# Two tap buffers, a later scan, an earlier start to the last tiles, and two moves in the head

## The chip, the cores and the metric

One core of a Trainium2 chip runs the kernel. The metric is the device time of one execution in microseconds (us), as the median of several runs; lower is better. The five engines are named as the profile names them: PE multiplies matrices (PEld is its weight load), ACT is the scalar engine, DVE the vector engine, POOL is GpSimd, and SP only issues transfers and waits.

## The reference

Two branches work on the same input `x` (2048 rows of 512) and are mixed row by row by a gate:

```python
g = sigmoid((x * gate_w).sum(-1, keepdims=True))
qkv = x @ wqkv                                   # 32 heads of 16
a = softmax(q @ k.T * 16 ** -0.5) @ v @ wo       # full attention, no mask
# b: a state-space convolution with 128 complex states per channel
K = einsum("dn,dnl,dn->dl", C, exp(dt * A * l), dt * B).real   # taps
b = irfft(rfft(u, 2L) * rfft(K, 2L))[:L] + u * Dskip           # u is x
out = g * a + (1 - g) * b
```

## The kernel before, in words

**Attention.** The scores are never stored. The loop `for q in range(NQ)` has 512 steps: 32 groups (a quarter of the rows and four heads), each with 16 key tiles. One step `q` computes four score products (`qk`, PE, into one of three double PSUM banks `SC`), two exponentials of 128x1024 (`ex(2q)` and `ex(2q+1)`, ACT, from `SC` into a ring of seven slots `ET`), and four products with the values (`pv`, PE, into the PSUM bank `OA`). `VE` holds the values, 17 columns a head, the 17th column is one, so that `OA` gets the sums of the softmax too; for that `VE` is filled with 1.0 before the values are written over it. After 16 steps `norm` (DVE) transposes `OA`, divides, and every second time writes a piece of `OnT`, the left operand of the output projection. So the kernel has 1,024 exponentials, all on ACT, and everything else is meant to run beside them.

**The convolution** is cut into 32 chunks of 64 rows and 16 blocks of 32 channels:
- `table` (DVE) makes two blocks' powers at a time into `PT` (two buffers), and sends them to DRAM (`ptd`).
- `qload` reads a block back transposed (`Qt`, a DMA transpose).
- `kstage` (PE, DVE) makes the taps of a block in the PSUM bank `MB`, copies them with zeros around them to the staging buffer `Kst` (two DVE instructions, L796 and L797), and sends that to DRAM (`kpd`). There is one `Kst` before.
- `sstage` (PE, DVE) makes the chunk states of a block, four banks one after the other in `MB`, each copied to `Sst` (L820, L822) and sent to DRAM (`sd`).
- `sload` reads the states of a block transposed into `SG0` or `SG1` (a quarter of the channels, four blocks, each).
- `scan` (DVE) runs over the 31 chunks of a quarter; five instructions for each, the first one (L861) copies from `SG` and so waits for its four loads.
- `ystage` (PE, DVE) computes 32 units of output in `MB` from `Py`, `Tt` (read back from `ptd` and `kpd` by `yload`) and `SG`, and copies them to `Yst`.
- `combine` and `outs` make output tiles 0 to 11 inside the loop; tiles 12 to 15 need the last group of heads and come behind it.

**What sets the order.** Every engine runs its own list of instructions in order. The lists are written by a recorder: one step `q` after the other, and within a step first the attention, then `sch.step(rate)`, which lets the threads above go on as far as they may. A thread yields conditions: `("PE", cost)` and `("DVE", cost)` take from a budget that each step refills (1.65 for DVE, 0.62 for PE in most of the loop), `("AFTER", name, n)` holds until `n` steps behind the step in which `name` was marked, and `("LOCK", "MB")` holds the one bank that `kstage`, `sstage`, `ystage`, `outs` and the projections share. This decides only an order; the real waits are semaphores that the recorder derives from who reads and writes which buffer. So an instruction that waits holds up all that stands behind it on its engine. SP issues all transfers of the loop, in the order of the recorded steps, the DMA transposes of `Qt`, `SG` and `Yl` among them.

**Head.** x rows 0 to 511 come by `x0n` and are transposed on PE (with the identity `idb`) into `xT`; the first K and Q projections, the first score products and the first exponential follow. The state-space parameters begin beside it (`ssm_head`, the same ACT).

Of the kernel before, what the change touches and what calls it, by code (L numbers as in the profile page):

```python
# [244 lines left out]
def declare(nc, es):  # L245
    B = {}

    def sb(name, free, dt=BF16):
        B[name] = Buf(name, "sb", free, dt)
# [30 lines left out]
    sb("Dpb", 16)  # L280
    sb("Dp", 16, FP32)
    sb("Yl", 16 * D)
    sb("fo", 2 * D)

    for n in ("AreT", "AimT", "BreT", "BimT", "CreT", "CimT", "ldt", "dt"):
        sb(n, D)
# [22 lines left out]
    sb("tt2", 2 * CB * 16)  # L309
    sb("Qt", 2 * 32 * 128)  # L310
    sb("Sst", 4 * 512)
    sb("Kst", 8 * P)

    sb("SG0", 33 * 2 * 128)
    sb("SG1", 33 * 2 * 128)
# [87 lines left out]
def dap(t, off, dims):  # L403
    return bass.AP(tensor=t, offset=off, ap=[list(d) for d in dims])


def record(nc, p, B, ins):
# [3 lines left out]
    OA, MB = B["OA"], B["MB"]  # L411
# [11 lines left out]
    def load(eng, b, src, W, dims=None, off=0):  # L423
        dma(eng, lambda e: e.dma_start(b(off, dims), src()), [], W)
# [22 lines left out]
    for c in range(1, 4):
        load_xT(c)
# [4 lines left out]
    for a in range(4):  # L453
# [7 lines left out]
    idf, idb, x0n = B["idf"], B["idb"], B["x0n"]  # L461
    op("POOL", lambda g: g.iota(idf(0, [[1, P]]), [[1, P]], base=0, channel_multiplier=-1,
                                allow_small_or_imprecise_dtypes=True), [], [(idf, 0)])
    op("POOL", lambda g: g.memset(VE(0, [[1, 16 * 560]]), 1.0), [], [(VE, k) for k in range(16)])
    wm = B["wm"]
    op("DVE", lambda v: v.memset(wm(0, [[1, D]]), 0.0), [], [(wm, 0)])
    op("DVE", lambda v: v.tensor_scalar(idb(0, [[1, P]]), idf(0, [[1, P]]), 0.0, None, ALU.is_equal), [(idf, 0)], [(idb, 0)])
    for k in range(6):
        mm(lambda: SC[2](0, [[1, 512]]), lambda: wm(0, [[1, 128]]), lambda: wm(0, [[1, 512]]), [(wm, 0)], [(SC[2], 0, "warm")])
    op("DVE", lambda v: v.memset(hpi(0, [[1, 1]]), HALF_PI), [], [(hpi, 0)])  # L470
    op("DVE", lambda v: v.memset(pio(1, [[1, 1]]), 0.0), [], [(pio, 1)])
# [76 lines left out]
    def norm(b):  # L548
        qc, pi, w = b // 8, (b % 8) // 2, b % 2
        o = 0  # L550
        op("DVE", lambda v: v.transpose(OT(o, [[1, 512]]), OA(0, [[1, 512]])), [(OA, 0, b)], [(OT, 0, b)])  # L551
        op("DVE", lambda v: v.reciprocal(Rz(16 * w, [[1, 16]]), OT(o + 16, [[32, 16]])), [(OT, 0, b)], [(Rz, w)])
        op("DVE", lambda v: v.tensor_tensor(ON(16 * w, [[32, 16], [1, 16]]), OT(o, [[32, 16], [1, 16]]),
                                            Rz(16 * w, [[1, 16], [0, 16]]), ALU.mult), [(OT, 0, b), (Rz, w)], [(ON, w)])
        if w == 1:
            op("DVE", lambda v: v.transpose(OnT[qc](pi * 512, [[1, 512]]), ON(0, [[1, 512]])), [(ON, 0), (ON, 1)],
               [(OnT[qc], 0)])


    def tt(eng, o, a, b_, f, R, W):  # L560
# [5 lines left out]
    def key(*ns):  # L566
        return [(B[n], 0) for n in ns]
# [210 lines left out]

    kpd, Kst = B["kpd"], B["Kst"]

    op("POOL", lambda g: g.memset(Kst(0, [[1, 8 * P]]), 0.0), [], [(Kst, "z")])

    def kstage(blk):
        yield ("AFTER", f"pt{blk}", 1)
        yield ("AFTER", "wb", 1)
        yield ("AFTER", "Dp", 1)
        yield ("LOCK", "MB")
        o = (blk % 2) * PTN
        for part, wn in ((0, "wrb"), (1, "nwi")):
            yield ("PE", .6)  # L790
            for a in range(4):
                mm(lambda a=a: MB(0, [[1, 512]], 32 * a, 32), lambda wn=wn: B[wn](CB * blk, [[1, 32]]),
                   lambda a=a, part=part: PT(o + part * CB * T + 512 * a, [[1, 512]]), [(PT, blk % 2, blk), (B[wn], 0)],
                   [(MB, 0, ('K', blk))], part == 0, part == 1, pos=(0, 32 * a))
        yield ("DVE", .7)
        op("DVE", lambda v: v.tensor_copy(Kst(63, [[P, 8], [1, T]]), MB(0, [[T, 8], [1, T]])), [(MB, 0, ('K', blk)), (Kst, "z")], [(Kst, 0, blk)])  # L796
        op("DVE", lambda v: v.tensor_scalar(Kst(63, [[P, 8]]), MB(0, [[T, 8]]), B["Dp"](blk, [[1, 1]]), None, ALU.add),  # L797
           [(MB, 0, ('K', blk)), (B["Dp"], 0)], [(Kst, 0, blk)])
        sch.unlock("MB")
        dma("SP", lambda e: e.dma_start(kpd.dram(blk * P * 8 * P, [[8 * P, P], [1, 8 * P]]), Kst(0, [[1, 8 * P]])),  # L800
            [(Kst, 0, blk), (Kst, "z")], [(kpd, blk)])
# [45 lines left out]
    def scan():  # L847
# [234 lines left out]
    for q in range(NQ):  # L1082
# [36 lines left out]
    while sch.thr:
        p.q += 1  # L1120
        sch.step(dict(PE=1e3, DVE=1e3, POOL=1e3))
        assert p.q < NQ + 3000, [t[1] for t in sch.thr]
# [38 lines left out]
```

## Time and profile before

| what | value |
|---|---|
| median of 3 runs | 1101.4 us (1099.38 to 1102.48) |
| the profiled execution, its own time | 1103.83 us |
| its span, first to last instruction | 1102.0 us |
| ACT busy | 981.1 us (89%) |
| PE busy | 756.7 us (69%) |
| DVE busy | 634.8 us (58%) |
| POOL busy | 10.2 us (1%) |
| mean granted TensorE clock | 0.61 of 2.4 GHz |

The profiled execution lies 2.4 us above the median of the runs, of which 1.8 us are outside its span. Shares of busy time are means over a head, a loop with very different stages, and a tail. The rows of the trace show each place apart.

### The profile page before, as it was taken

What the parts mean: (1) busy time and instruction counts of PE and PEld (TensorE: products, weight loads), DVE (VectorE), ACT (ScalarE), POOL (GpSimd) and SP (SyncE); (2) the same over time, 40 slices, a digit from 0 to 9 for tenths busy, and PEclk for the clock granted to TensorE, in tenths of its full rate; (3) what the DMA queues carried; (4) which work ended last, traced back from release to release, by engine and by line L of the source; (5) the groups of instructions that cost most, each with busy time, mean ns of one, the idle gap of its engine ahead of it and who ended that gap; (6) DMA issues with size and microseconds to landing.
All of it is one profiled execution on the core that took longest, in us unless ns stands there. A gap on an engine that the chain in (4) does not pass through costs nothing.

```text
span 1102.0 us, 16304 instructions
## 1 busy us (share of the span) xinstructions
PE 756.7 (69%) x6614; PEld 211.7 (19%) x6614; DVE 634.8 (58%) x1354; ACT 981.1 (89%) x1042; POOL 10.2 (1%) x12
## 2 busy tenths in 40 slices
PE   6867667667566674666656648885877888877665
PEld 2211112111111111111111113332322333311111
DVE  6738889976549975399864521107968951131201
ACT  5999999998779987899888959995997999999995
POOL 3000000000000000000000000000000000000000
PEclk9988985555555556555566655555555555568856
DMA  8700000036580036800347562354464334100000
GB/s 167 154 1 1 1 1 1 1 111 176 134 229 21 1 107 143 227 22 1 106 105 211 151 175 73 85 130 94 105 125 104 85 89 94 38 17 24 20 1 20
DMA packets 227403, 92.17 MB, mean 84 GB/s; under 512 B 191872, under 2 KB 215040, under 8 KB 225280
## 3 DMA queue, kind: packets, MB, share of 16 engines
q1 hardware_dynamic: 224016, 88.90, 32.5%
q10 hardware_dynamic: 3312, 2.23, 1.0%
q8 instruction: 52, 0.85, 0.3%
q14 instruction: 23, 0.19, 0.1%
HBM read 27.92 MB, written 35.65 MB: 58 GB/s over the span
## 4 chain that ended last, share of the span: by engine, by line
ACT 43%; DVE 30%; PE 11%; SPq 8%; DMA 5%; issue 2%; ACTq 0%; DVEq 0%; POOL 0%; POOLq 0%
ACT ET L536 42%; PE MB L420 5%; DVE G L871 4%; SPq L773 4%; PE SC L420 4%; DVE s L864 3%; DVE s L866 3%; DVE s L869 3%; DVE SG L873 3%; DMA gm_kpd<-Kst 2%; DVE tt L561 2%; PE OA L420 2%; SPq L841 2%; DMA gm_sd<-Sst 2%; DVE OT L551 1%
## 5 line engine op out<-in xcount | busy, mean ns | idle before, releaser
L536 ACT ACTIVATE ET<-SC 128x1024 bf16<-128x1024 f32 x1024 | 966.2, 1109 | 98.3 <-PE SC L420 97.3
L420 PE MATMUL SC<-Qm,KT 32*128 32x512 bf16 x2048 | 289.6, 556 | 204.5 <-ACT ET L536 198.2
L420 PE MATMUL OA<-ET,VE 128*32 128x512 bf16 x2048 | 287.6, 565 | 1.3 <-ACT ET L536 1.2
L420 PEld LDWEIGHTS SC<-Qm,KT 32*128 32x128 bf16 x2048 | 54.6, 97 | 407.6 <-ACT ET L536 391.0
L420 PEld LDWEIGHTS OA<-ET,VE 128*32 128x32 bf16 x2048 | 53.8, 101 | 190.3 <-issue 184.0
L420 PE MATMUL MB<-Qt,X 64*32 64x256 bf16 x512 | 39.9, 404 | 70.6 <-DVE Kst L797 44.5
L551 DVE STREAM_TRANSPOSE OT<-OA 128x512 f32<-128x512 f32 x32 | 23.8, 743 | 88.2 <-PE OA L420 88.2
L931 DVE CAST Yst<-MB 128x256 bf16<-128x256 f32 x32 | 13.4, 418 | 101.0 <-PE MB L420 101.0
L561 DVE TENSOR_TENSOR tt<-B,D 128x1024 bf16<-128x1024 bf16 x96 | 62.0, 688 | 1.3
L420 PE MATMUL MB<-Py,SG 128*32 128x64 bf16 x1024 | 59.8, 314 | 2.3 <-issue 2.3
L796 DVE CAST Kst<-MB 128x512 bf16<-128x512 f32 x16 | 11.0, 689 | 82.5 <-DMA gm_kpd<-Kst 70.4
L820 DVE CAST Sst<-MB 128x256 bf16<-128x256 f32 x64 | 27.0, 422 | 53.3 <-PE MB L420 48.9
L871 DVE TENSOR_TENSOR G<-s,s 128x256 f32<-128x256 f32 x120 | 53.2, 444 | 4.1
L420 PE MATMUL MB<-Tt,X 64*32 64x64 bf16 x512 | 35.6, 267 | 27.9 <-DVE Yst L931 27.9
L864 DVE TENSOR_TENSOR s<-G,MU 128x256 f32<-128x256 f32 x120 | 52.8, 440 | 0.1
L866 DVE TENSOR_TENSOR s<-G,MU 128x256 f32<-128x256 f32 x120 | 52.6, 438 | 0.0
L869 DVE TENSOR_TENSOR s<-s,SG 128x256 f32<-128x256 f32 x120 | 51.9, 432 | 0.0
L420 PEld LDWEIGHTS MB<-Py,SG 128*32 128x32 bf16 x1024 | 42.8, 222 | 10.5 <-issue 2.5
L873 DVE CAST SG<-G 128x256 bf16<-128x256 f32 x120 | 36.1, 301 | 4.1
L420 PEld LDWEIGHTS MB<-Tt,X 64*32 64x32 bf16 x512 | 19.0, 135 | 82.3 <-issue 82.1
L561 DVE TENSOR_TENSOR PT<-tt,tt 128x1024 bf16<-128x1024 bf16 x48 | 33.2, 691 | 1.5
L561 DVE TENSOR_TENSOR ft<-FP,L 128x1024 f32<-128x1024 f32 (+1 forms) x32 | 33.7, 1085 | 0.4
(119 smaller groups left out, 419.4 us busy)
## 6 DMA issues: line engine op xcount, KB each, us to landing
gm_ptd<-PT SPq DMA_DIRECT2D x16, 1024.0 KB, 5.2
Py<-gm_ptd SPq DMA_DIRECT2D x32, 512.0 KB, 4.4
gm_sd<-Sst SPq DMA_DIRECT2D x64, 128.0 KB, 2.5
gm_kpd<-Kst SPq DMA_DIRECT2D x16, 256.0 KB, 2.6
Tt<-gm_kpd SPq DMA_DIRECT2D x128, 32.0 KB, 3.5
gm_xrd<-in_A_x_dram SPq DMA_DIRECT2D x1, 2048.0 KB, 12.5
X<-gm_xrd SPq DMA_DIRECT2D x8, 256.0 KB, 5.1
gm_ytd<-Yst SPq DMA_DIRECT2D x32, 64.0 KB, 1.8
```

Source lines behind the costliest of these rows:

```text
L420: op("PE", lambda t: t.matmul(out(), lhsT(), rhs(), start=start, stop=stop, skip_group_check=True, **kw), R, W)
L536: op("ACT", lambda a: a.activation(ET(1024 * e, [[1, 1024]]), sc(0, [[1, 1024]]), AF.Exp, scale=DH ** -0.5), [(sc, 0, h // 2), (sc, 1, h / ...
L551: op("DVE", lambda v: v.transpose(OT(o, [[1, 512]]), OA(0, [[1, 512]])), [(OA, 0, b)], [(OT, 0, b)])
L561: op(eng, lambda v: v.tensor_tensor(o(), a(), b_(), f), R, W)
L773: dma("SP", lambda e: e.dma_start_transpose(Qt((blk % 2) * PTN, [[128, 32], [1, 128]]), ptd.dram(blk * P * PTN, [[PTN, P], [1, PTN]])), [( ...
L820: op("DVE", lambda v, bank=bank: v.tensor_copy(Sst(512 * bank, [[256, 2], [1, 128]]), MB(0, [[256, 2], [1, 128]])), [(MB, 0, ('S', blk, ba ...
L841: dma("SP", lambda e: e.dma_start_transpose(sg(256 + CB * bl, [[128, 64], [1, CB]]), sd.dram(CB * blk * 8192, [[8192, CB], [1, 8192]])), [ ...
L864: op(e, lambda v: v.tensor_tensor(s2(0, [[128, 2], [1, 128]]), G(0, [[128, 2], [1, 128]]), MU(d0, [[0, 2], [1, 128]]), ALU.mult), key("G", ...
L866: op(e, lambda v: v.tensor_tensor(s3(0, [[128, 2], [1, 128]]), G(128, [[-128, 2], [1, 128]]), MU(D + d0, [[D, 2], [1, 128]]), ALU.mult), k ...
L869: op(e, lambda v, so=so: v.tensor_tensor(s2(0, [[1, 256]]), s2(0, [[1, 256]]), sg(so, [[1, 256]]), ALU.add), [(s2, 0)] + ks, [(s2, 0)])
L871: op(e, lambda v: v.tensor_tensor(G(0, [[1, 256]]), s2(0, [[1, 256]]), s3(0, [[1, 256]]), ALU.add), [(s2, 0), (s3, 0)], [(G, 0)])
L873: op(e, lambda v, so=so: v.tensor_copy(sg(so, [[1, 256]]), G(0, [[1, 256]])), key("G"), ks)
```

## The change

It has five parts.
1. `Kst` gets a second buffer: block `blk` uses half `blk % 2`. `kstage` starts three steps behind the table of its block, where it was one.
2. `scan` starts a quarter twelve steps behind the issue of the quarter's last `SG` load, where it was four.
3. Output tiles 12 to 15: the first three of their four partial products are issued before the last group is finished, in the bank `MB` and in banks of `SC`; the fourth follows behind the last `norm`. `fo`, from which the tiles are sent out, has four buffers, where it had two. Each piece of `OnT` is tracked apart. What is left of the threads is run out inside step 511.
4. The loads of `Wv` and of the later columns of `Wk` and `Wq` are issued by SP, between its transposes, where ACT issued them.
5. In the head, `VE` is filled by DVE, where POOL did it; PE gets nine warming products, where it had six; K's first evacuation is done by DVE behind `Qm`, where ACT did it.

```diff
-    sb("fo", 2 * D)
+    sb("fo", 4 * D)
-    sb("Kst", 8 * P)
+    sb("Kst", 2 * 8 * P)
...
-    load_w("Wv", 2 * D, 0, D, 0)
-    load_w("Wk", D, P, D - P, 1)
-    load_w("Wq", 0, P, D - P, 1)
     load_par("AreT", ins["are"])
     load_par("AimT", ins["aim"])
-    for c in range(1, 4):
-        load_xT(c)
+    load_w("Wv", 2 * D, 0, D, 0, "SP")
+    load_xT(1)
+    load_w("Wk", D, P, D - P, 1, "SP")
+    load_w("Wq", 0, P, D - P, 1, "SP")
+    load_xT(2)
+    load_xT(3)
...
-    op("POOL", lambda g: g.memset(VE(0, [[1, 16 * 560]]), 1.0), [], [(VE, k) for k in range(16)])
     op("DVE", lambda v: v.memset(wm(0, [[1, D]]), 0.0), [], [(wm, 0)])
     op("DVE", lambda v: v.tensor_scalar(idb(0, [[1, P]]), idf(0, [[1, P]]), 0.0, None, ALU.is_equal), [(idf, 0)], [(idb, 0)])
-    for k in range(6):
+    op("DVE", lambda v: v.memset(VE(0, [[1, 16 * 560]]), 1.0), [], [(VE, k) for k in range(16)])
+    for k in range(9):
...
-    op("POOL", lambda g: g.memset(Kst(0, [[1, 8 * P]]), 0.0), [], [(Kst, "z")])
+    op("POOL", lambda g: g.memset(Kst(0, [[1, 16 * P]]), 0.0), [], [(Kst, "z")])
...
-        yield ("AFTER", f"pt{blk}", 1)
+        yield ("AFTER", f"pt{blk}", 3)
...
-        op("DVE", lambda v: v.tensor_copy(Kst(63, [[P, 8], [1, T]]), MB(0, [[T, 8], [1, T]])), [(MB, 0, ('K', blk)), (Kst, "z")], [(Kst, 0, blk)])
+        op("DVE", lambda v: v.tensor_copy(Kst(1024 * (blk % 2) + 63, [[P, 8], [1, T]]), MB(0, [[T, 8], [1, T]])), [(MB, 0, ('K', blk)), (Kst, "z")], [(Kst, blk % 2, blk)])
...
-                yield ("AFTER", f"sg{4 * qr + bl}", 4)
+                yield ("AFTER", f"sg{4 * qr + bl}", 12)
...
-    proj_ev("K", 0, 0, mb, True)
...
     op("DVE", lambda v: v.tensor_scalar(Qm(0, [[1, 512]]), OA(0, [[1, 512]]), msk(0, [[1, 1]]), None, ALU.mult),
        [(OA, 0, ('p', "Q", 0, 0)), (msk, 0)], [(Qm, 0, 0)])
+    proj_ev("K", 0, 0, mb)
...
+    p.q = max(p.q, NQ)
+    banks = [(MB, 0, 0), (SC[(2 * NQ - 3) % 3], 0, 0), (SC[(2 * NQ - 3) % 3], 512, 1), (SC[(2 * NQ - 2) % 3], 0, 0)]
+    for i in range(3):
+        for pi in range(3):
+            out_mm(12 + i, banks[i], pi)
+    pv(NQ - 1)
+    for pi in range(3):
+        out_mm(15, banks[3], pi)
     norm(31)
...
-    banks = [(OA, 0, 0), (SC[0], 0, 0), (SC[1], 0, 0), (SC[2], 0, 0)]
     for i in range(4):
-        for _ in outproj(12 + i, banks[i], False):
+        for _ in outproj(12 + i, banks[i], [3], False):
             pass
```

Where the recorder puts things is seen in the lists of the engines. The first place is SP at the first pair of blocks (`gm_ptd<-PT` sends a table, `gm_kpd<-Kst` the taps, `Qt<-gm_ptd` reads a table back, `gm_sd<-Sst` sends states). Before:

```order
L761 DMA gm_ptd<-PT 128x4096 x2
L800 DMA gm_kpd<-Kst 128x1024
L773 DMA_TRANSPOSE Qt<-gm_ptd 128x32x128 x2
L800 DMA gm_kpd<-Kst 128x1024
L761 DMA gm_ptd<-PT 128x4096 x2
```

Of the change:

```order
L762 DMA gm_ptd<-PT 128x4096 x2
L774 DMA_TRANSPOSE Qt<-gm_ptd 128x32x128 x2
L801 DMA gm_kpd<-Kst 128x1024 x2
L762 DMA gm_ptd<-PT 128x4096 x2
L827 DMA gm_sd<-Sst 128x2x256 x4
```

Both sends of taps now stand behind the two transposes; before, the first stood ahead of them and the second behind.

The second place is DVE where the scan of the third quarter begins (`G<-SG` is its first instruction, which waits for the four loads; `Yst<-MB` evacuates a unit of output). Before, the loads were issued on SP in step 339, behind the unit that the row L931 ahead of the scan evacuates, and the scan began in step 343:

```order
L556 STREAM_TRANSPOSE OnT_59<-ON 128x512
L931 CAST Yst<-MB 128x256 x3
L519 TENSOR_SCALAR Qm<-Q_52,msk 128x512
L931 CAST Yst<-MB 128x256
L551 STREAM_TRANSPOSE OT<-OA 128x512
L552 RECIPROCAL Rz<-OT 128x16
L553 TENSOR_TENSOR ON<-OT,Rz 128x16x16
L931 CAST Yst<-MB 128x256
L861 CAST G<-SG_136 128x256
L864 TENSOR_TENSOR s_139<-G,MU 128x256
```

Of the change, the loads are issued in step 337, and the scan begins in step 349:

```order
L557 STREAM_TRANSPOSE OnT_59<-ON 128x512
L932 CAST Yst<-MB 128x256 x3
L520 TENSOR_SCALAR Qm<-Q_52,msk 128x512
L932 CAST Yst<-MB 128x256
L552 STREAM_TRANSPOSE OT<-OA 128x512
L553 RECIPROCAL Rz<-OT 128x16
L554 TENSOR_TENSOR ON<-OT,Rz 128x16x16
L932 CAST Yst<-MB 128x256 x3
L520 TENSOR_SCALAR Qm<-Q_52,msk 128x512
L932 CAST Yst<-MB 128x256
L862 CAST G<-SG_136 128x256
L865 TENSOR_TENSOR s_139<-G,MU 128x256
```

Three more units are evacuated between the loads and the scan's first instruction.

The third place is DVE at the start of the program (`idb` is the identity, `hpi`, `piota` and `msk` are small constants, `xT<-SC` are the first copies that PE's projections wait for). Before:

```order
L466 MEMSET wm 128x256
L467 TENSOR_SCALAR idb<-idf 128x128
L470 MEMSET hpi 128x1
L471 MEMSET piota 128x1
L473 SCALAR_TENSOR_TENSOR piota<-piota 128x1 x7
L477 MEMSET msk 128x2
L479 SCALAR_TENSOR_TENSOR msk<-piota,msk 128x1 x4
L481 TENSOR_SCALAR msk<-msk 128x1
L1058 CAST xT<-SC 128x512 x2
```

Of the change:

```order
L466 MEMSET wm 128x256
L467 TENSOR_SCALAR idb<-idf 128x128
L468 MEMSET VE 128x8960
L471 MEMSET hpi 128x1
L472 MEMSET piota 128x1
L474 SCALAR_TENSOR_TENSOR piota<-piota 128x1 x7
L478 MEMSET msk 128x2
L480 SCALAR_TENSOR_TENSOR msk<-piota,msk 128x1 x4
L482 TENSOR_SCALAR msk<-msk 128x1
L1063 CAST xT<-SC 128x512 x2
```

The fill of `VE` now stands ahead of everything that DVE does for the first exponential, apart from `idb`. The tables of blocks 6 and 7 and of 10 and 11 also change places with the scans of the first and second quarter: they are finished in steps 157 and 221 (before: 186 and 252), ahead of the scans. The last tile made inside the loop, number 11, is recorded in step 487 of 512 (before: 481).

## Rows read from the trace of the kernel before

**Rows 1.** The page's groups: line, engine, tiles, count; busy, mean ns; idle before.

```profile
L536 ACT ACTIVATE ET<-SC 128x1024 bf16<-128x1024 f32 x1024 | 966.2, 1109 | 98.3 <-PE SC L420 97.3
```

**Rows 2.** ACT's timeline: start us, us, instruction, count, idle before and releaser.

```profile
252.04 14.77 ACT L536 ACTIVATE ET<-SC 128x1024 bf16<-128x1024 f32 x16 [5.01 <-PE SC L420]
...
332.49 69.77 ACT L536 ACTIVATE ET<-SC 128x1024 bf16<-128x1024 f32 x76 [5.32 <-PE SC L420]
...
652.26 11.11 ACT L536 ACTIVATE ET<-SC 128x1024 bf16<-128x1024 f32 x12 [11.64 <-PE SC L420]
...
752.92 8.15 ACT L536 ACTIVATE ET<-SC 128x1024 bf16<-128x1024 f32 x8 [8.76 <-PE SC L420]
...
833.10 8.07 ACT L536 ACTIVATE ET<-SC 128x1024 bf16<-128x1024 f32 x8 [7.32 <-PE SC L420]
```

**Rows 3.** Waits: who for whom, us in total, times, longest.

```profile
DVE Kst L796 <- DMA gm_kpd<-Kst: 70.4, 8, 15.4
PE MB L420 <- DVE Kst L797: 46.6, 8, 11.9
DVE G L861 <- DMA SG<-gm_sd: 29.2, 2, 16.8
PE MB L420 <- DVE Sst L822: 20.1, 21, 2.0
```

**Rows 4.** Timeline at the first pair of blocks, and SP's at 630 us.

```profile
241.38 11.98 SPq L773 DMA_TRANSPOSE Qt<-gm_ptd  x2
245.80 0.69 DVE L796 CAST Kst<-MB 128x512 bf16<-128x512 f32 x1 [5.76 <-DMA gm_kpd<-Kst]
250.81 0.65 PE L420 MATMUL MB<-Qt,X 64*32 64x256 bf16 x8 [6.08 <-DVE PT L561]
...
630.93 2.59 SPq L895 DMA_DIRECT2D Tt<-gm_kpd  x4
```

**Rows 5.** DMA issues: tiles, queue, count, median us from issue to landing.

```profile
Qt<-gm_ptd SPq DMA_TRANSPOSE x16, 7.5
```

**Rows 6.** Timeline of the head.

```profile
0.86 0.27 DVE L466 MEMSET wm<- 128x256 uint32 x1 [0.86 <-PEq L1146]
1.08 7.57 POOL L464 MEMSET VE<- 128x8960 bf16 x1
1.18 7.55 DVE L467 TENSOR_SCALAR idb<-idf 128x128 bf16<-128x128 f32 x1
8.59 1.03 POOL L781 MEMSET Kst<- 128x1024 bf16 x1
11.01 1.28 DVE L1058 CAST xT<-SC 128x512 bf16<-128x512 f32 x2
15.45 0.75 DVE L1067 TENSOR_SCALAR Qm<-OA,msk 128x512 bf16<-128x512 f32 x1 [1.23 <-PE OA L420]
16.56 0.56 ACT L507 CAST KT<-MB 128x512 bf16<-128x512 f32 x1
17.73 1.89 PE L420 MATMUL MB<-Wv,xT 128*128 128x512 bf16 x4
18.44 3.77 ACT L536 ACTIVATE ET<-SC 128x1024 bf16<-128x1024 f32 x4
20.40 1.04 PE L420 MATMUL MB<-Wv,xT 128*128 128x512 bf16 x4 [0.24 <-DVE VE L502]
```

**Rows 7.** Timeline of the tail.

```profile
1089.44 0.62 PE L420 MATMUL OA<-ET,VE 128*32 128x512 bf16 x4 [1.16 <-ACT ET L536]
1092.45 1.89 PE L420 MATMUL OA<-Wo,OnT 128*128 128x512 bf16 x4 [2.39 <-DVE OnT L556]
1098.53 0.75 DVE L1016 SCALAR_TENSOR_TENSOR fo<-SC,g,Yl 128x512 bf16<-128x512 f32 x1 [0.82 <-DMA out_dram<-fo]
```

**Rows 8.** Windows: stretch, busy us (count) of PE, PEld, DVE, ACT, POOL; PEclk, DMA share, GB/s.

```profile
337.00:366.00 29.00, 18.43 (x128) 3.44 (x128) 27.87 (x80) 29.00 (x33) 0.00 (x0) 0.50 0.00 1
685.00:714.00 29.00, 24.84 (x287) 9.80 (x284) 3.65 (x7) 29.00 (x30) 0.00 (x0) 0.50 0.41 102
```

More of the change, by code (lines that the diff above doesn't have):

```diff
@@ L433, in load_par, with load_w @@
         dma(q, lambda e: e.dma_start_transpose(B[n](0, [[1, D]]), src), [], [(B[n], 0)])
-    def load_w(n, c0, at, cols, sl):
-        load("ACT", B[n], lambda: dap(w_t, c0 + at, [[3 * D, P], [P * 3 * D, 4], [1, cols]]), [(B[n], sl)], [[D, 4], [1, cols]], at)
+    def load_w(n, c0, at, cols, sl, eng="ACT"):
+        load(eng, B[n], lambda: dap(w_t, c0 + at, [[3 * D, P], [P * 3 * D, 4], [1, cols]]), [(B[n], sl)], [[D, 4], [1, cols]], at)
     load("ACT", B["x0n"], lambda: dap(x_t, 0, [[D, P], [P * D, 4], [1, D]]), [(B["x0n"], 0)], [[D, 4], [1, D]])
@@ L556, in norm @@
             op("DVE", lambda v: v.transpose(OnT[qc](pi * 512, [[1, 512]]), ON(0, [[1, 512]])), [(ON, 0), (ON, 1)],
-               [(OnT[qc], 0)])
+               [(OnT[qc], pi)])
     def tt(eng, o, a, b_, f, R, W):
@@ L795, in kstage @@
         yield ("DVE", .7)
-        op("DVE", lambda v: v.tensor_copy(Kst(63, [[P, 8], [1, T]]), MB(0, [[T, 8], [1, T]])), [(MB, 0, ('K', blk)), (Kst, "z")], [(Kst, 0, blk)])
-        op("DVE", lambda v: v.tensor_scalar(Kst(63, [[P, 8]]), MB(0, [[T, 8]]), B["Dp"](blk, [[1, 1]]), None, ALU.add),
-           [(MB, 0, ('K', blk)), (B["Dp"], 0)], [(Kst, 0, blk)])
+        op("DVE", lambda v: v.tensor_copy(Kst(1024 * (blk % 2) + 63, [[P, 8], [1, T]]), MB(0, [[T, 8], [1, T]])), [(MB, 0, ('K', blk)), (Kst, "z")], [(Kst, blk % 2, blk)])
+        op("DVE", lambda v: v.tensor_scalar(Kst(1024 * (blk % 2) + 63, [[P, 8]]), MB(0, [[T, 8]]), B["Dp"](blk, [[1, 1]]), None, ALU.add),
+           [(MB, 0, ('K', blk)), (B["Dp"], 0)], [(Kst, blk % 2, blk)])
         sch.unlock("MB")
-        dma("SP", lambda e: e.dma_start(kpd.dram(blk * P * 8 * P, [[8 * P, P], [1, 8 * P]]), Kst(0, [[1, 8 * P]])),
-            [(Kst, 0, blk), (Kst, "z")], [(kpd, blk)])
+        dma("SP", lambda e: e.dma_start(kpd.dram(blk * P * 8 * P, [[8 * P, P], [1, 8 * P]]), Kst(1024 * (blk % 2), [[1, 8 * P]])),
+            [(Kst, blk % 2, blk), (Kst, "z")], [(kpd, blk)])
         sch.mark(f"K{blk}")
@@ L1004, in record, with out_mm, outproj @@
     fo, Wo = B["fo"], B["Wo"]
-    def outproj(lt, bank, steps=True):
+    def out_mm(lt, bank, pi):
         b, off, sl = bank
         qc, r = divmod(lt, 4)
-        for pi in range(4):
+        mm(lambda: b(off, [[1, 512]]), lambda: OnT[qc](pi * 512 + 128 * r, [[1, 128]]), lambda: Wo(pi * D, [[1, D]]),
+           [(OnT[qc], pi), (Wo, 0)], [(b, sl, ('o', lt))], pi == 0, pi == 3)
+    def outproj(lt, bank, pis, steps=True):
+        b, off, sl = bank
+        for pi in pis:
             if steps:
                 yield ("PE", .45)
-            mm(lambda: b(off, [[1, 512]]), lambda pi=pi: OnT[qc](pi * 512 + 128 * r, [[1, 128]]), lambda pi=pi: Wo(pi * D, [[1, D]]),
-               [(OnT[qc], 0), (Wo, 0)], [(b, sl, ('o', lt))], pi == 0, pi == 3)
+            out_mm(lt, bank, pi)
         if steps:
             yield ("DVE", .75)
-        op("DVE", lambda v: v.scalar_tensor_tensor(fo((lt % 2) * D, NAT), b(off, NAT), B["g"](lt, [[1, 1]]),
+        op("DVE", lambda v: v.scalar_tensor_tensor(fo((lt % 4) * D, NAT), b(off, NAT), B["g"](lt, [[1, 1]]),
                                                    Yl(lt * D, PERM), ALU.mult, ALU.add),
-           [(b, sl, ('o', lt)), (Yl, ("c", lt))] + key("g"), [(fo, lt % 2)])
-        dma("SP", lambda e: e.dma_start(dap(ins["out"], 128 * lt * D, [[D, P], [1, D]]), fo((lt % 2) * D, [[1, D]])),
-            [(fo, lt % 2)], [(B["d_out"], lt)])
+           [(b, sl, ('o', lt)), (Yl, ("c", lt))] + key("g"), [(fo, lt % 4)])
+        dma("SP", lambda e: e.dma_start(dap(ins["out"], 128 * lt * D, [[D, P], [1, D]]), fo((lt % 4) * D, [[1, D]])),
+            [(fo, lt % 4)], [(B["d_out"], lt)])
     def outs():
@@ L1027, in outs @@
             yield ("LOCK", "MB")
-            yield from outproj(lt, (MB, 0, 0))
+            yield from outproj(lt, (MB, 0, 0), range(4))
             sch.unlock("MB")
@@ L1114, in record @@
         sch.step(rate)
-    q = NQ
-    p.q = q
-    pv(q - 1)
-    norm(31)
[L1119 to L1122, printed above, removed]
-    banks = [(OA, 0, 0), (SC[0], 0, 0), (SC[1], 0, 0), (SC[2], 0, 0)]
+        if q == NQ - 1:
+            while sch.thr:
+                p.q += 1
+                sch.step(dict(PE=1e3, DVE=1e3, POOL=1e3))
+                assert p.q < NQ + 3000, [t[1] for t in sch.thr]
+    p.q = max(p.q, NQ)
[6 more added lines that the diff above has]
+        out_mm(15, banks[3], pi)
+    norm(31)
     for i in range(4):
-        for _ in outproj(12 + i, banks[i], False):
+        for _ in outproj(12 + i, banks[i], [3], False):
             pass
```

## Prediction

> **What bounds the kernel now.** I read the page's groups first. ACT's exponentials are busy 966.2 of 1102 us and idle for 98.3 us ahead of one, of which 97.3 end with a score product of PE [rows 1]. So ACT sets the pace, and what can be won in the loop is those 98 us. ACT's timeline says where they lie and what an exponential costs where nothing waits: 76 of them run in 69.77 us, 0.918 each [rows 2], which is 1.84 us a step. An exponential's own row is 1.109 us [rows 1], so neighbours overlap by 0.19 us, and a gap costs 0.19 us more than it shows.
>
> Ten gaps carry most of the loss. Eight lie between 252 us (5.01) and 652 us (11.64): 5.01, 6.25, 5.32, 7.15, 4.76, 4.30, 1.62 and 11.64, in sum 46.1 us, and the first, the third and the last of them stand in [rows 2]. The other two are 8.76 us at 752.9 and 7.32 us at 833.1 [rows 2].
>
> The list of waits says what is behind them. DVE's copy into `Kst` waits 8 times, 70.4 us in all, for the send of the block before to leave the one buffer; PE's next product in `MB` waits 8 times, 46.6 us, for that copy [rows 3]. PE takes its list in order, so the next score product stands behind and ACT runs dry. The two later gaps are of the same make: the first instruction of a scan waits twice, 29.2 us in all, for `SG` [rows 3], the evacuations of the output units stand behind it on DVE, PE's next unit behind these, and the scores behind that.
>
> **The change, part by part.**
>
> *Second tap buffer.* The eight gaps with their lost overlap are 46.1 + 8 x 0.19 = 47.6 us. A copy now waits for a send of a pair before, 14 steps or more back, and so for nothing. What comes next in each place decides what is kept.
> - First pair: `Kst` was done before 247 us, yet PE went on only at 250.81 [rows 4], so something else released it: the transposed load of `Qt`, issued at 241.38 and, at the median of 7.5 us to landing, due at 248.9 [rows 4, 5]. The transposes do not move, since they wait for the table. PE comes one step later (1.84 us), so of its wait of 6.08 us there remain 2.4 (landing at 248.9) to 4.2 us (at 250.8). I take 3.3; ACT saw 1.1 us less than PE, so **2.2 us** stay.
> - Last pair: SP issues three `Py` loads and twelve small loads in one go, four of which take 2.59 us [rows 4], some 10 us in sum, ahead of the sends of block 13's states, the last `Qt`, and the sends of block 14. The copies of the states (`Sst`, four banks) wait for these sends. Counting from the table's send in steps of 1.84 us, with 5 us for a `Qt` issue, block 14's first copy comes about 1 us and block 15's first product and copy another 1 to 2 us too early. **2.0 us** stay; bounds 0 and 6 (half of the 11.64).
> - Elsewhere PE waits for a copy that is only on its way. **1.0 us** for all, between 0 and seven times 0.4.
>
> Kept: 47.6 - 5.2 = **42.4 us**.
>
> *Scan twelve steps behind.* The four loads took at most 16.8 us [rows 3] beyond step four; twelve steps are 22 us. Both gaps go: 8.76 + 7.32 + 2 x 0.19 = **16.5 us**. The work behind it moves 5 or 6 steps back, and the last tile of the loop from step 481 to 487 of 512, so 25 steps still cover it. Without that cover, each of its tiles would come behind the last exponential, at four products (1.89) and an evacuation (0.75) [rows 7], 2.6 us a tile.
>
> *What the new order adds.* Where a block's first three state banks follow a table in one step, each product waits for the copy of the one before: 21 such waits are 20.1 us [rows 3], a PE wait of about 1 us each, and it takes two in a row before ACT shows it. Blocks 4 and 8 now do this too, and block 5's first product stands behind the end of a scan. **2.4 us** lost; bounds 0 and 6.
>
> *Head.* DVE's identity `idb` should be short, but it took 7.55 us, from 1.18 to 8.73, and ended 0.08 us behind POOL's fill of `VE` (1.08 to 8.65) [rows 6]: the one held up the other. That fill leaves POOL, but the next one there, `Kst`, is twice as long now: 2 x 1.03 us [rows 6], so `idb` ends at about 3.2. Then DVE fills `VE`. The only DVE fill of any size to price it by is `wm`, 0.27 us for 256 words of four bytes [rows 6]. By elements, 8960 of them cost 9.45 us; by bytes, half: 4.7. I take the elements, since the list of the change has 8960 of them while `wm`'s 512 values stand as 256 words: a fill of ones was not packed. [...]
>
> So the fill ends at 12.65 and, with the 2.28 us of small constants that stood between `idb` and the copies of `xT` (8.73 to 11.01), these begin at 14.9, **3.9 us later** [rows 6]. ACT no longer copies `KT` (0.56 us), so its queue is 3.4 us late; PE's first score product needs `Qm` and now `KT` behind it on DVE: 15.45 + 3.9 + 0.75 + 0.7 = 20.8, where `KT` was ready at 17.12 [rows 6]. PE's side is the later one: **3.7 us**. The three loads that leave ACT's queue gain nothing, since ACT then waits for DVE. A V projection took 1.89 us at 17.7 and 1.04 us at 20.4, TensorE's two clock levels [rows 6]; PE now idles from the transposes to 15 us, so some of the first projections may still run at the lower level: 0.8 us, at most 3. Head: **+4.5 us**; bounds -1 (by bytes) and +6.7.
>
> *Tail.* Nine of the products of tiles 12 to 14 now stand on PE ahead of the last value products, which could run at 1089.44 before, 1.16 us after PE went idle [rows 7]. At the tail's rate, four in 1.89 us, of which the last 0.2 is drain, or 0.43 each [rows 7], nine take 3.85 us: the last values come 2.7 us later. Behind them the last `norm` is as long as it was, and then one product with its drain (0.65) and four evacuations of 0.75 with some 0.05 between, 3.9 us to the end of the last, where it was 6.9 (1092.4 to 1099.28) [rows 7]. Gain 0.35 us; bounds 2.3 (PE at its upper clock) and a loss of 1.
>
> *Sum.* -42.4 - 16.5 + 2.4 + 4.5 - 0.35 = -52.4, from the profiled execution's 1103.8: 1051.4. That execution lies 2.4 us above the median, so the forecast is **1049 us**.
>
> **The rivals.**
> - *SP is the real limit.* The two transposes of a pair hold SP for 11.98 us [rows 4], and the first gap was already released by one. If half of each of the eight gaps comes back as a wait for `Qt` or `sd`, 23 us return: 1072. Against it: 8 waits for the copy itself are 46.6 us [rows 3], so seven gaps ended with it. Chance 0.10.
> - *The fill goes by bytes.* Then `xT` is copied at 10.2, 0.8 us earlier than before, and the head is 0.5 to 1 us shorter in place of 4.5 longer: 1044. Nothing but the packing of `wm` speaks against it. [...] Chance 0.10.
> - *Slower: the clock.* Without pauses, PE stays at its lower level. If then the stretch of the tables (some 400 exponentials between 200 and 650 us) became PE-bound, as where output units run (30 exponentials in 29 us at 0.50 of the clock [rows 8]), it would cost 0.05 us each, 20 us in all. It decides from 0.13 us each, 52 us: then the time is the old one, and at 0.16 it is 1113. Against it: 33 exponentials in 29 us beside a scan at the same 0.50 [rows 8]. Chance 0.02.
> - *Nothing is won,* since DVE, freed of its waits, is late elsewhere (a scan holds it 27.87 of 29 us [rows 8]) and all 46 and 16 us turn up as other waits: 1101. Chance 0.02.
>
> **How the numbers follow.** The forecast has 0.76. About 0.3% (3 us) is what a measurement can tell here from no change. The first two rivals are faster as well: faster 0.96, same 0.02, slower 0.02. Range: the lower end takes the head by bytes and half of the other low bounds, 1040; the upper end adds the upper bounds of the remains (4 and 4 us), of the new bank waits (3) and part of the clock, 1061. SP's case stays outside.
>
> **What the profile after must show.** No wait of L796's successor for `gm_kpd` nor of the scan's first instruction for `SG`; ACT's idle time ahead of exponentials at 40 to 50 us, of which 2 at the first pair (ended by `Qt`); on DVE a fill of about 9.4 us and the first exponential near 22 us; nine products ahead of the last values, and some 12 us from the end of the last exponential to the span's end, as before. The prediction is wrong if gaps of over 3 us stand at the later pairs, if the fill is short, or if exponentials without gaps need over 0.95 us between 250 and 650 us.

## The result and the profile after

The changed kernel takes **1044.2 us** (median of 4 runs, 1042.3 to 1046.3) beside 1101.8 us (4 runs, 1099.4 to 1102.5) of the kernel before, a ratio of 0.948 (95% interval 0.946 to 0.951). It is faster, as forecast, by 57.7 us where 52.4 were forecast; the time lies inside the range. The profiled execution took 1042.3 us; its span is 1040.5, 61.5 less than that of before. Every execution of either kernel takes 1.8 us more than its span, so the 1.8 us are no part of the 2.4 us by which the profiled one of before lies above its median; the profiled one of the change lies 1.8 us below its own.

The page's group of the exponentials answers to [rows 1]:

```profile
L537 ACT ACTIVATE ET<-SC 128x1024 bf16<-128x1024 f32 x1024 | 963.9, 1110 | 40.0 <-PE SC L420 39.0
```

ACT does the same work in the same time and stands idle ahead of it for 40.0 us, 58.3 less.

The list of waits (who for whom, us in total, times, longest) has no row any more in which `Kst` waits for `gm_kpd`, PE for `Kst` for more than half a microsecond, or `G` for `SG` [rows 3]. What stands at their place:

```profile
ACT ET L537 <- PE SC L420: 39.0, 30, 3.5
PE MB L420 <- DVE Sst L823: 22.1, 17, 3.8
PE MB L420 <- DVE Yst L932: 8.4, 5, 2.3
DVE Sst L821 <- DMA gm_sd<-Sst: 7.4, 2, 3.7
```

ACT's timeline from 240 to 620 us, where [rows 2] had its first three gaps and five more (start, us, instruction, count, idle before it):

```profile
248.51 14.77 ACT L537 ACTIVATE ET<-SC 128x1024 bf16<-128x1024 f32 x16 [1.53 <-PE SC L420]
264.43 33.11 ACT L537 ACTIVATE ET<-SC 128x1024 bf16<-128x1024 f32 x36 [1.15 <-PE SC L420]
...
333.07 56.94 ACT L537 ACTIVATE ET<-SC 128x1024 bf16<-128x1024 f32 x62 [1.21 <-PE SC L420]
393.46 1.94 ACT L537 ACTIVATE ET<-SC 128x1024 bf16<-128x1024 f32 x2 [3.45 <-PE SC L420]
...
518.41 1.94 ACT L537 ACTIVATE ET<-SC 128x1024 bf16<-128x1024 f32 x2 [3.45 <-PE SC L420]
...
605.52 5.60 ACT L537 ACTIVATE ET<-SC 128x1024 bf16<-128x1024 f32 x6 [1.45 <-PE SC L420]
613.05 1.94 ACT L537 ACTIVATE ET<-SC 128x1024 bf16<-128x1024 f32 x2 [1.93 <-PE SC L420]
```

Of the eight gaps of 46.1 us there remain the first pair's 1.53 and the last pair's 1.45 and 1.93. Two gaps of 3.45 us are new. Between gaps 62 exponentials run in 56.94 us and 36 in 33.11, 0.92 each, as before.

At the first pair, the timeline of SP and PE and the list of the `Qt` loads:

```profile
239.49 10.87 SPq L774 DMA_TRANSPOSE Qt<-gm_ptd  x2
247.70 0.45 PE L420 MATMUL MB<-Qt,X 64*32 64x256 bf16 x8 [2.47 <-issue]
DMA to landing us min/median/max: 8.1/8.4/8.7
```

The first transpose landed 8.1 us after its issue, at 247.6, and PE went on at 247.70 (its row names no releaser): this gap is still ended by `Qt`.

The head, to be laid beside [rows 6]:

```profile
1.08 1.81 POOL L782 MEMSET Kst<- 128x2048 bf16 x1
1.18 1.79 DVE L467 TENSOR_SCALAR idb<-idf 128x128 bf16<-128x128 f32 x1
3.22 7.53 DVE L468 MEMSET VE<- 128x8960 bf16 x1 [0.25 <-issue]
13.01 1.28 DVE L1063 CAST xT<-SC 128x512 bf16<-128x512 f32 x2
18.87 1.04 PE L420 MATMUL MB<-Wv,xT 128*128 128x512 bf16 x4
19.95 3.77 ACT L537 ACTIVATE ET<-SC 128x1024 bf16<-128x1024 f32 x4
24.58 3.84 ACT L537 ACTIVATE ET<-SC 128x1024 bf16<-128x1024 f32 x4 [0.86 <-PE SC L420]
```

`idb` again ends beside POOL's fill, the short one of `Kst` now. The fill of `VE` took 7.53 us on DVE, the copies of `xT` came 2.0 us later than before, the first exponential 1.5 us.

The tail, to be laid beside [rows 7] (the last exponential ends at 1030.25):

```profile
1029.07 1.46 PE L420 MATMUL MB<-Wo,OnT 128*128 128x512 bf16 x3
1030.32 1.50 PE L420 MATMUL SC<-Wo,OnT 128*128 128x512 bf16 x6
1031.76 0.40 PE L420 MATMUL OA<-ET,VE 128*32 128x512 bf16 x4
1033.78 0.71 DVE L557 STREAM_TRANSPOSE OnT<-ON 128x512 bf16<-128x512 bf16 x1
1035.04 0.75 DVE L1021 SCALAR_TENSOR_TENSOR fo<-MB,g,Yl 128x512 bf16<-128x512 f32 x1 [0.55 <-PE MB L420]
1035.71 2.06 DVE L1021 SCALAR_TENSOR_TENSOR fo<-SC,g,Yl 128x512 bf16<-128x512 f32 x3
```

Nine products stand ahead of the last value products, and the four evacuations follow one another without a wait for a send; 10.25 us pass from the last exponential's end to the span's end, where it was 12.6.

### The profile page after: what moved, and what is told of

Same layout as the page of the kernel before. It is cut to its first block, busy times and chain, and to the rows that moved or that the text cites. A ratio compares the mean times of both kernels' runs of the same rounds, so it can differ in the third digit from the quotient of the medians.

```text
span 1040.5 us, 16316 instructions
## 1 busy us (share of the span) xinstructions
PE 752.9 (72%) x6617; PEld 212.2 (20%) x6617; DVE 636.2 (61%) x1356; ACT 978.2 (94%) x1041; POOL 3.5 (0%) x11
## 4 chain that ended last, share of the span: by engine, by line
ACT 57%; DVE 27%; PE 12%; issue 2%; SPq 1%; DMA 1%; DVEq 0%; POOL 0%; POOLq 0%
ACT ET L537 56%; PE MB L420 6%; DVE G L872 4%; PE SC L420 4%; DVE s L870 4%; DVE s L867 3%; DVE s L865 3%; DVE SG L874 3%; PE OA L420 2%; DVE VE L503 1%; DVE OT L552 1%; SPq L896 1%; DVE VE L468 1%; DVE Sst L821 1%; DVE KT L510 1%
## 5 line engine op out<-in xcount | busy, mean ns | idle before, releaser
L420 PE MATMUL MB<-Qt,X 64*32 64x256 bf16 x512 | 39.3, 398 | 27.2 <-DVE Sst L823 22.1
L1021 DVE SCALAR_TENSOR_TENSOR fo<-MB,g,Yl 128x512 bf16<-128x512 f32 x13 | 9.7, 747 | 55.2 <-PE MB L420 55.2
```

The lines of the kernel that those rows point to most:

```text
L420: op("PE", lambda t: t.matmul(out(), lhsT(), rhs(), start=start, stop=stop, skip_group_check=True, **kw), R, W)
```

## The experiments

Each is timed beside the kernel before on the same chip (medians of before 1100.5 to 1102.9 us); gains are against that median. "Loop" is the time from the start of the 229th exponential (ahead of the first pair) to that of the last, read from each trace: it leaves out head and tail, whose clock differs from one execution to the next (last section). "Idle" is ACT's idle time ahead of exponentials on the page.

| kernel | median us | ratio to before (95%) | idle us | loop us |
|---|---|---|---|---|
| before | 1101.8 | 1 | 98.3 | 843.2 |
| changed kernel | 1044.2 | 0.948 (0.946 to 0.951) | 40.0 | 785.9 |
| two buffers alone | 1077.3 | 0.979 (0.977 to 0.981) | 70.6 | 817.0 |
| scan twelve steps alone | 1084.4 | 0.986 (0.984 to 0.989) | 81.2 | 822.2 |
| two buffers, taps three steps | 1075.2 | 0.975 (0.973 to 0.978) | 71.7 | 816.9 |
| two buffers, scan twelve steps | 1049.9 | 0.953 (0.951 to 0.956) | 47.9 | 789.4 |
| change, one buffer | 1081.7 | 0.983 (0.981 to 0.985) | 78.4 | 822.6 |
| change, taps one step | 1051.6 | 0.954 (0.952 to 0.955) | 47.9 | 790.5 |
| change, products last | 1043.9 | 0.949 (0.947 to 0.951) | 43.8 | 784.5 |
| change, small fill | 1038.1 | 0.943 (0.941 to 0.944) | 41.3 | 783.8 |
| change, fill on POOL | 1044.4 | 0.949 (0.947 to 0.950) | 42.7 | 784.2 |
| change, one bank a step | 1028.2 | 0.934 (0.932 to 0.936) | 26.3 | 770.3 |
| change, small fill and one bank a step | 1021.6 | 0.928 (0.926 to 0.929) | 24.1 | 769.5 |

The loops of the four kernels that differ from the change only in head and tail, its own among them, lie between 783.8 and 785.9.

**Two buffers alone.** The kernel before with the second tap buffer and nothing else.

```diff
-    sb("Kst", 8 * P)
+    sb("Kst", 2 * 8 * P)
...
-            [(Kst, 0, blk), (Kst, "z")], [(kpd, blk)])
+            [(Kst, blk % 2, blk), (Kst, "z")], [(kpd, blk)])
```

> The kernel before with nothing but the second tap buffer (taps still one step behind their table). If the one buffer made the eight gaps of 46 us: seven go, the first keeps 2 to 5 us and the last pair some 3, so 1060 us (1055 to 1066), and no copy into Kst waits for a send. If SP's queue is the limit and the buffer only hid it: half of the gaps comes back as waits for Qt or for the sends of the states, 1078 to 1085. If the later start of the taps did the work and not the buffer: 1095 or more.

Measured: 1077.3 us, a gain of 23 where the prediction's working gives 42: outside the 1055 to 1066 of the first theory, and just under the rival's 1078 to 1085. In the list of waits of this kernel the wait for `gm_kpd` is gone, but the scan's wait for `SG`, in two places before [rows 3], is in four, and ACT waits for value products as well:

```profile
ACT ET L536 <- PE SC L420: 64.2, 42, 8.7
DVE G L861 <- DMA SG<-gm_sd: 39.8, 4, 16.8
DVE Sst L820 <- DMA gm_sd<-Sst: 13.6, 5, 4.3
ACT ET L536 <- PE OA L420: 5.5, 4, 1.5
```

The scans of the first two quarters, which had waited for nothing, now wait 5.97 and 4.82 us. Before, SP issued the last load of the first one at 327.6 us and DVE reached the scan at 332.9, behind the gap of 5.32 us that stood there [rows 2]; now DVE is there at 318.7, ahead of the load's issue at 319.8 and its landing at 324.7. The gap that was removed had covered the load; five gaps of ACT beside them make 6.5 us. The first pair keeps 4.53 us where the working leaves 2.2, and the last pair 2.05, 1.63 and 3.90 where it leaves 2.0. With the lost overlap of the five (0.19 each) that is 15 of the 19 us that are missing.

**Scan twelve steps alone.**

```diff
-                yield ("AFTER", f"sg{4 * qr + bl}", 4)
+                yield ("AFTER", f"sg{4 * qr + bl}", 12)
```

> The kernel before with nothing but the scan twelve steps behind its loads. If the scan's wait for SG made the gaps of 8.8 and 7.3 us: both go, and where the scans of the first two quarters now end ahead of a block of states, 2 to 6 us come back, so 1086 to 1092 us. If the stretch of the output units is bound by PE and takes the time back: 1097 to 1102.

Measured: 1084.4 us, 16 us less, as the sum has it (16.5); by the loops it is 21.1. It lies below the 1086 to 1092 expected: of the 2 to 6 us that were to come back nothing is seen. No wait of `G` for `SG` is left in its list.

**Both, taps still one step behind the table.** The edits of the two kernels above together, which tells whether the two gains add up.

> The kernel before with the second tap buffer and the scan twelve steps behind its loads; the taps still start one step behind their table, head and tail as before. In the run with the buffer alone the first instruction of the scans of the first two quarters waited for SG too (5.97 and 4.82 us, before 0), and ACT showed five gaps beside these scans (1.00, 1.20, 1.54, 1.20, 1.55 us). Theory that these waits only moved from the taps to the scan: with twelve steps they go as well as the 16.1 us of the two later scans, so 1077 - 17 - 7 = 1053 us (1050 to 1056), and no wait of the scan for SG is left. Rival, SP's queue is the limit and the waits turn up again elsewhere: the sum of the two single changes, 1101.5 - 24 - 16.5 = 1061 us (1059 to 1064).

Measured: 1049.9 us, 52.4 less than before. The first theory holds, and more (1 us under its 1050 to 1056): alone the two give 23 and 16 us, together 52. No wait of `G` for `SG` is in this trace, and what is left there is

```profile
ACT ET L536 <- PE SC L420: 46.8, 34, 5.1
PE MB L420 <- DVE Sst L822: 21.9, 16, 3.6
DVE Sst L820 <- DMA gm_sd<-Sst: 9.6, 3, 4.6
```

By the loops the surplus is smaller: 26.3 and 21.1 alone, 53.8 together, 6.4 more than the sum. Either way the buffer's worth hangs on the scan's distance.

**The change with one buffer.** The counterpart: everything of the change but the second buffer.

```diff
-        op("DVE", lambda v: v.tensor_copy(Kst(1024 * (blk % 2) + 63, [[P, 8], [1, T]]), MB(0, [[T, 8], [1, T]])), [(MB, 0, ('K', blk)), (Kst, "z")], [(Kst, blk % 2, blk)])
+        op("DVE", lambda v: v.tensor_copy(Kst(63, [[P, 8], [1, T]]), MB(0, [[T, 8], [1, T]])), [(MB, 0, ('K', blk)), (Kst, "z")], [(Kst, 0, blk)])
...
```

> The changed kernel with one tap buffer again, all else kept, the start three steps behind the table too. If the buffer is what counts: the copies wait for the sends again, and since both sends of a pair now stand behind its transposed loads on SP, for as long as before or longer: 1084 to 1096 us. If the later start is what counts: 1044 to 1050.

Measured: 1081.7 us, 2 us under the expected 1084 to 1096. Taken out of the whole change, the buffer is worth 39 us (0.9832 less 0.9481 of 1102; by the loops 36.7), and the wait is back, though not longer than before (70.4 us, the longest 15.4):

```profile
DVE Kst L797 <- DMA gm_kpd<-Kst: 66.9, 8, 14.4
```

**Two buffers, taps three steps behind the table.** Part 1 of the change as a whole, without the scan: the edits of the first experiment and this one.

```diff
-        yield ("AFTER", f"pt{blk}", 1)
+        yield ("AFTER", f"pt{blk}", 3)
```

> The kernel before with the second tap buffer and the taps three steps behind their table (the whole of part 1 of the change), the scan still four steps behind its loads, head and tail as before. With the buffer and one step the first pair kept a gap of 4.53 us, and the last pair kept 2.05, 1.63 and 3.90. Theory that the taps' sends and products stood too near the table's transposes: the first gap becomes 1.5 and the last pair's 3.4 as in the change, so 1077 - 3 - 4 = 1070 us (1067 to 1073). Rival, the two further steps do nothing: 1077 us (1075 to 1079).

Measured: 1075.2 us, 2 us less than with one step (4 by the ratios to before), and the same loop (816.9 and 817.0): the rival holds for the time. In ACT's timeline the first pair does gain (2.13, beside 4.53 with one step, 1.5 foreseen), and up to the last pair this kernel is 3.2 us ahead in its loop. The last pair takes back 0.8 of them, and the stretch behind it, that of the output units, the rest; why was not followed up. The first pair, and the longest gap at the last:

```profile
250.27 14.77 ACT L536 ACTIVATE ET<-SC 128x1024 bf16<-128x1024 f32 x16 [2.13 <-PE SC L420]
...
636.98 3.77 ACT L536 ACTIVATE ET<-SC 128x1024 bf16<-128x1024 f32 x4 [6.66 <-PE SC L420]
```

**The change with the taps one step behind the table.** The same number, set back in the whole change.

> The changed kernel with one number set back: the taps start one step behind their table, as before the change, where they start three behind. Question: whether the 5.7 us between the buffer with the later scan (1049.9) and the whole change (1044.2) come from these two steps. Theory that they do for the most part: with one step the first pair shows a gap of 5.13 us, with three 1.53, so about 4 us come back: 1047.5 to 1050. Rival, the two steps are worth little, as in the run with the buffer and the three steps but the early scan (1075.2 beside 1077.3), and the rest is head and tail: 1043.5 to 1046.

Measured: 1051.6 us, 1.6 us beyond the theory's 1047.5 to 1050, so the two steps are worth about 6 us here (0.9535 less 0.9481 of 1102), 4.5 by the loops. The gap at the first pair is 4.45 us again:

```profile
253.58 14.77 ACT L537 ACTIVATE ET<-SC 128x1024 bf16<-128x1024 f32 x16 [4.45 <-PE SC L420]
```

This kernel and the one with buffer and scan differ only in parts 3 to 5: 0.9535 and 0.9534, each known to 0.0024 or better. These parts together come to nothing that can be measured so; part 4, the warming products and K's evacuation were not tried alone.

**All products of the tail behind the last values.** The four buffers and the banks stay.

```diff
-    for i in range(3):
-        for pi in range(3):
-            out_mm(12 + i, banks[i], pi)
     pv(NQ - 1)
-    for pi in range(3):
-        out_mm(15, banks[3], pi)
     norm(31)
     for i in range(4):
-        for _ in outproj(12 + i, banks[i], [3], False):
+        for _ in outproj(12 + i, banks[i], range(4), False):
```

> The changed kernel with all sixteen products of the last four tiles behind the last norm, as before; banks and the four output buffers kept. By the prediction's working (PE at its lower clock, 2.7 us of delay for the last values against 3.0 won behind them) it is within 0.5 us: 1044 to 1045. If the 2.4 us by which the tail is shorter come from the early products, with the clock risen under them: 1046 to 1047.5.

Measured: 1043.9 us, no difference. The profiled executions show one: the tail takes 11.5 us here (the last exponential ends at 1034.02, the span at 1045.56) and 10.25 in the change. The change itself has both tails: with the taps one step behind, whose tail is the same code, the profiled one takes 11.6 us as well, its six products in `SC` 2.77 us at a granted clock of 0.50, where those of the change take 1.50 at 1.00. So 1.3 of the 2.4 us by which the profiled tail is shorter than that of before are the clock that PE had in that execution. The other 1.1, between this tail and the 12.6 of before, go with what is kept of part 3. Three products of tile 12 still run beside the norm, though they are recorded behind it, since each piece of `OnT` is tracked apart (the first row; the norm's last piece is written from 1036.31 on); and the evacuation that stood behind a send [rows 7] waits for PE now (the second row):

```profile
1034.62 1.46 PE L420 MATMUL MB<-Wo,OnT 128*128 128x512 bf16 x3
1039.50 0.75 DVE L1021 SCALAR_TENSOR_TENSOR fo<-SC,g,Yl 128x512 bf16<-128x512 f32 x1 [0.95 <-PE SC L420]
```

**Filling only what must be one.** `VE` is filled in its columns of ones and its padding alone, 512 and 256 elements a partition; the values write the rest.

```diff
-    op("DVE", lambda v: v.memset(VE(0, [[1, 16 * 560]]), 1.0), [], [(VE, k) for k in range(16)])
+    op("DVE", lambda v: v.memset(VE(16, [[560, 16], [17, 32]]), 1.0), [], [(VE, k) for k in range(16)])
+    op("DVE", lambda v: v.memset(VE(544, [[560, 16], [1, 16]]), 1.0), [], [(VE, k) for k in range(16)])
```

> The changed kernel, with VE filled only where no value is ever written: 512 columns of ones and 256 columns of padding instead of 8960 elements, on DVE. If the fill on DVE holds up the first exponential (7.5 us, first exponential at 19.95): the copies of xT begin at 6 to 7 us instead of 13, the first exponential at 13.5 to 15, and the time falls by 4 to 6.5 us: 1038 to 1040. If the loads or the tables of ACT hold the head: first exponential at 18 or later, 1042 to 1044.

Measured: 1038.1 us, 6 less, as expected. The head's timeline:

```profile
0.86 0.27 DVE L466 MEMSET wm<- 128x256 uint32 x1 [0.86 <-PEq L1158]
3.11 0.48 DVE L468 MEMSET VE<- 128x512 bf16 x1
3.72 0.27 DVE L469 MEMSET VE<- 128x256 bf16 x1
3.94 0.06 DVE L472 MEMSET hpi<- 128x1 f32 x1
...
13.20 3.77 ACT L538 ACTIVATE ET<-SC 128x1024 bf16<-128x1024 f32 x4
```

256 elements take 0.27 us as two-byte ones and as four-byte words, one element takes 0.06: these fills go by elements, with a fixed part, at 0.82 ns an element between 256 and 512 and 0.83 between 512 and the 8960 of the change (7.53 us). The Trainium skill says that a memset takes one cycle per element whatever its type (VectorE: DVE Perf Modes, section Zero memsets can be issued as uint32); that the type makes no difference, the two rows of 0.27 us bear out.

**The fill back on POOL.** The line of the fill moves to POOL, ahead of `wm`.

> The changed kernel with the whole fill of VE back on POOL, as before. If POOL's fill holds up the identity until 8.7 us as it did: xT at 11, first exponential at 17.9 (two us earlier than with the fill on DVE, since the constants of DVE no longer stand behind 9.7 us of fills), the time 1 to 2 us less: 1042 to 1043. If the move of the fill was a gain: 1045 to 1047.

Measured: 1044.4 us, between the two expected ranges and no different from the change, so no worth of the move can be measured, although ACT starts 2.0 us sooner here. ACT's timeline of this kernel:

```profile
17.95 3.77 ACT L537 ACTIVATE ET<-SC 128x1024 bf16<-128x1024 f32 x4
24.71 1.94 ACT L537 ACTIVATE ET<-SC 128x1024 bf16<-128x1024 f32 x2 [2.99 <-PE SC L420]
```

A window of PE in the head (stretch, busy us and count, granted clock, DMA share, GB/s), of this kernel and then of the change:

```profile
19.00:22.00 3.00, 2.43 (x8) 0.50 0.57 122
```

```profile
19.00:22.00 3.00, 1.87 (x11) 1.00 0.43 95
```

PE's second V projection took 1.89 us here and 1.04 in the change, the scores stand behind it, and the fifth exponential starts at 24.71 and 24.58: the two microseconds are gone in this execution. That they are in the timed ones too is likely from the medians, not shown.

**One state bank a step.** This kernel starts the products of a block's four state banks one to a step, where in the change the first three come in one; the last tile made inside the loop then comes in step 509 of 512.

```diff
             yield ("LOCK", "MB")
+            yield ("Q", p.q + 1)
             yield ("PE", .6)
```

> The changed kernel, with every state product one step behind the lock of its bank, so no two products of states stand in one step (last tile of the loop in step 509 instead of 487). If the remaining gaps of 1.2 us (ten) and 3.45 us (two) come from PE waiting for a copy that stands behind other work on DVE: they go, 12 to 18 us, so 1027 to 1033. If PE waits for the transposed loads or the sends instead: 1040 or more. Cost if the 509 is too late: some us at the end.

Measured: 1028.2 us, 16 less. The waits for `Sst`, the largest group left in the change, fall from 22.1 us in 17 places to

```profile
ACT ET L537 <- PE SC L420: 25.0, 27, 1.9
PE MB L420 <- DVE Sst L824: 8.7, 6, 2.2
```

**Both together.** The small fill and one bank a step.

> Both of the two before that are meant to gain: the small fill and one state product a step. If they are independent: the sum of the two gains, 1021 to 1028. If the shorter head is taken back at the first pair (its transposed load is not earlier): 3 to 5 us of it are missing.

Measured: **1021.6 us** (1020.5 to 1023.3), 0.928 of the time before: they add up (6 and 16, 22.6 together), and this is the fastest version found. Of its 24.1 us of idle time, one gap is over 2 us, 3.08 at 626 us, at the last pair.

## Why the prediction was right, and where it was wrong

The sign, the main mechanism (waits for the one tap buffer and for `SG` that starve ACT) and the time of the whole were right. Taken apart by the profiled executions, the span's 61.5 us are 1.8 up to the 229th exponential, 57.3 in the loop and 2.4 behind the last.

- *Pairs:* 46.1 us of gaps became 1.53, 1.45 and 1.93. With the overlap, 47.6 - 4.9 - 3 x 0.19 = 42.1, where 42.4 were forecast. First pair 1.5 (forecast 2.2), ended by `Qt` as said; last pair 3.4 (forecast 2.0, within the bounds 0 to 6); elsewhere nothing (forecast 1.0).
- *Scans:* both gaps are gone, 16.5 as forecast. The cover was misread: 16.8 us of waiting beyond step four were set against the 22 us of all twelve steps, but only eight are added, 14.7 us. It sufficed by little in the kernel with the later scan alone: the last load of the third scan was issued at 732.88, loads land 4.8 us after their issue at the median, and the scan began at 738.56.
- *New order:* the gaps of over 0.3 us that end with an `Sst` copy and are not counted above rose from 15.8 to 18.4 us, 2.6; 2.4 were forecast. One of the two gaps of 3.45 us is that of block 5, whose first product stands behind the end of a scan, as named; the other is that of block 9, which has the same place behind the second scan and was not named.
- The remaining 1.3 us of the loop are smaller gaps, not forecast.
- *Head:* forecast +4.5. The first exponential came at 19.95, not near 22, the fifth 0.95 us later than before (24.58 and 23.63), and with smaller gaps behind it the 229th 1.8 us sooner. That is this execution's luck: in the five profiled executions with this head the 229th starts between 243.2 and 248.4 us, in the five with the head of before between 243.8 and 247.0, 0.9 us sooner on the mean. **Here a step failed:** the fill was priced at 0.27 us for 256 elements, 9.45 us, without the fixed part of about 0.06 us that the row of a single element shows. With it: (0.27 - 0.06) / 256 = 0.82 ns an element, 7.4 us; 7.53 was measured. So `xT` came 2.0 us late and not 3.9, and the V projections were at the upper clock in this execution, for which 0.8 had been added. The rival by bytes (4.7 us) is refuted.
- *Tail:* forecast -0.35, in the profiled execution -2.4; the low bound, PE at its upper clock, was 2.3. The last values were to come 2.7 us later; from the last exponential's end to their start there are 0.05 us before, 1.5 here, where the clock rose, and 2.8 in the kernel with the taps one step behind, at the lower clock. Behind them 8.8 us pass in both, where it was 12.6: 3.8 were won where 3.0 were priced. At the lower clock the early products so won nothing (11.6 us of tail with them, 11.5 without), and the timed medians show no gain either.

Two of the prediction's own signs of being wrong appeared. Gaps of over 3 us stand at later pairs, two of 3.45 us, though behind `Sst` copies and not behind `Kst`; and the fill took 7.53 us where some 9.4 were named, though not the 4.7 of the rival by bytes.

**The step that the runs overturned is the independence of the terms.** The sum gave 42.4 us to the buffer. Alone it gives 23, on top of the rest 39. What it frees at the pairs is partly lost at the scans of the first two quarters, because a gap at the pair had covered the loads of `SG`, and without it DVE comes to the scan before SP has issued the last of them; twelve steps cover that, four do not. The prediction priced these steps at the two scans that waited before, and these alone. The forecast held because the change makes both edits; that was luck, since the working never asked what the one does to the other. The two steps of the taps hang on it too: about 6 us with the later scan (4.5 by the loops), without it 2 by the medians and none by the loops.

The rival "SP is the real limit" had its 1072 nearly met by the buffer alone (1077): a queue's loads did become the next wait, those of `SG`, not those of `Qt`. In the whole change it is wrong: PE waits for `Qt` 2.5 us at the first pair and 2.2 at the last, and the copies 7.4 us for `sd`. The rival of the clock is wrong too: 36 exponentials in 33.11 us from 264 us on and 62 in 56.94 from 333 show none of the 0.05 us each that it wanted.

## What to carry to other kernels

A wait that is removed brings the work behind it forward, and every distance in steps that was long enough before may be too short then: look for the next transfer in the chain that does not come sooner, and price the removal together with it. When parts of a change are to be credited, set one back in the whole as well as making it alone; here that read 39 and 23 us for the same buffer. Price a fill or a copy from two rows of different length, so that its fixed part shows.

## What the hardware showed that was not expected

TensorE's clock differs between executions at the same place of the same code. With the head of before, the fifth exponential started at 23.6 to 23.7 us (before, two buffers alone, two buffers with taps at three steps) or at 25.2 (scan alone, buffer and scan); with the head of the change at 24.6 in its own execution, at 25.3 to 26.7 with one buffer, one bank a step and the products last, and at 26.7 with the taps one step behind, where the window from 22 to 25 us has a granted clock of 0.50, and 1.00 in the other (columns as in [rows 8]; first the one step, then the change):

```profile
22.00:25.00 3.00, 1.81 (x5) 0.57 (x5) 0.69 (x1) 1.73 (x2) 0.00 (x0) 0.50 0.36 65
```

```profile
22.00:25.00 3.00, 1.76 (x10) 0.41 (x8) 1.44 (x3) 2.14 (x3) 0.00 (x0) 1.00 0.33 44
```

These are the two levels, 1.2 and 2.4 GHz. Head and tail together so carry some 3 us that belong to no edit; what decides the level was not settled.
